# Zero products during the first loads, value copies on another engine, later turns: one edit of a window-attention and expert kernel

## The chip, the cores and the metric

The kernel runs on one core of a Trainium2 chip. The metric is the device time of one execution in microseconds, taken as the median of three runs. Before the change that is 1030.5 us (1030.44 to 1033.13). The core's engines are TensorE (PE), VectorE (DVE), ScalarE (ACT), GpSimd (POOL) and SyncE (SP), which issues most transfers. Each engine works through its own queue in a fixed order and waits on semaphores.

## The reference

The inputs are q, k and v of shape 8 x 8 x 576 x 64 (batch, heads, positions, width), float32, and the weights of one gated expert. What is computed:

```
scores = (q @ k^T) / sqrt(64)        # per batch and head
scores = where(0 <= i - j < 64, scores, -1e9)
attn   = softmax(scores)             # + 1e-9 in the denominator
x      = (attn @ v) as 4608 tokens x 512
xn     = x / sqrt(mean(x*x) + 1e-6) * rms_g
g, val = xn @ w_gate, xn @ w_val     # 512 x 1536 each
out    = (g * sigmoid(g) * val) @ w_out   # 1536 x 512
```

## The kernel before

Tokens are worked in nine tiles of 512. The attention of a batch is done in four pairs of heads (so pairs 0 to 3 are batch 0, 4 to 7 batch 1, 8 to 11 the third batch). The expert's products take each float32 operand as a sum of two f16 parts, three products for one (`three`, lines 790 to 792: high by high, high by low, low by high). Before a weight block can be used it is widened, scaled and split (lines 205 to 236); before a token tile can be used, its high part is cast on ACT (line 746) and its low part is made on POOL (line 748).

The first two batches go through `scores` (line 386 products, line 399 masks on DVE, line 402 exponentials on ACT, lines 469 and 470 sums, lines 474 and 476 scaling on POOL), `weights_to_keys` (line 489 transposes on PE, lines 492 and 494 copies) and `attention_values` (line 507). From the third batch on the scaling and the transpose go another way: POOL moves 32x32 blocks (`move`, line 371, 16 instructions for a pair) and DVE turns them (`turn`, lines 374 and 375), so the turn of a pair waits for its moves.

Values are needed in two layouts, from an even and an odd block. For batch 0 one transfer brings the even layout, and two copies on DVE (lines 342 and 343) make the odd one in the same tile; for later batches two more transfers bring it.

The largest of `rms_g` sets a scale (`rms_weights`, lines 174 to 186): a small transfer, a maximum on DVE (line 175), a PE transpose (`gps`, line 177), another maximum (line 178), and a PE broadcast (`gpb`, line 181).

What stands in which queue when is decided twice. The program emits its parts by planned due times (half steps of the expert's loop; `attention_events` gives those of the attention, and line 598 those of the turns). Then a scheduler that goes by modelled times orders the instructions of each engine. An edit at one place can thus move instructions at others. From tile 1, block 3 on the order is that in which the program emits.

Of the kernel before, what the change touches and what calls it, by code (L numbers as in the profile page):

```python
# [14 lines left out]
F32 = mybir.dt.float32  # L15
F16 = mybir.dt.float16
BF16 = mybir.dt.bfloat16
# [8 lines left out]
P = 128  # L26
B, H, S, D = 8, 8, 576, 64
NPAIR = H // 2
NBLK = S // D
NKT = 5  # L30
# [3 lines left out]
TT = 512  # L34
# [5 lines left out]
NST, T2K, F4K, NKV, NPT, NQ = 3, 8, 6, 3, 3, 3  # L40
LT0, LV0 = 1.4, 2.6
VISITS = (27, 32, 37, 42.5, 47.5)
MOVES = (8.7, 7, 4.5, 4)
FIRST7 = NT
ORDERED = (1, 3)
PREP0, PREP1 = 32.2, 55.5
ST = 2 * NBLK * P - D
# [9 lines left out]
def tile_window_attention_moe(  # L57
# [10 lines left out]
    nc = tc.nc  # L68

    cp = ctx.enter_context(tc.tile_pool(name="cp", bufs=1))  # L70
    wk = ctx.enter_context(tc.tile_pool(name="wk", bufs=2))
# [5 lines left out]
    ps_mo = early.enter_context(tc.tile_pool(name="ps_mo", bufs=3, space=PSUM))  # L77
# [32 lines left out]
    def plus_minus(t):  # L110
        nc.vector.tensor_copy(t[:, 0, :], ident)
        nc.vector.tensor_scalar(t[:, 1, :], ident, -1.0, None, ALU.mult)

    plus_minus(unit)
    one = cp.tile([P, 1], F32, name="one")
    nc.vector.memset(one, 1.0)
    ones = one.to_broadcast([P, P])
# [208 lines left out]
    def load_kv(n):  # L326

        if n == 3:
            kvt = wk.tile([P, 2, NKD, TT], F16, tag="xn", name=f"kv_{n}")
            kvt = kvt.rearrange("p a b c -> p (a b c)").bitcast(F32)[:, : S + NBLK * P]  # L330
        else:
            kvt = wk.tile([P, S + NBLK * P], F32, tag="kv", name=f"kv_{n}", bufs=NKV)
        if n < NPAIR:
            nc.sync.dma_start(out=kvt[:, :S], in_=kv[n, :, :S])
        else:
            nc.sync.dma_start(out=kvt[:, : S + NKT * P], in_=kv[n])
        even = kvt[:, S : S + NKT * P].rearrange("p (u c) -> p u c", c=P)
        odd = kvt[:, S + NKT * P :].rearrange("p (u c) -> p u c", c=P)

        def values_in():  # L340
            nc.sync.dma_start(out=kvt[:, S : S + NKT * P], in_=kv[n, :, S : S + NKT * P])
            nc.vector.tensor_copy(odd[0:D], even[0:D, : NKT - 1, :])
            nc.vector.tensor_copy(odd[D:P], even[D:P, 1:, :])

        if n < NPAIR:
            later[n] = values_in
        else:
            src = kv[n, :, S : S + NKT * P].rearrange("p (u c) -> p u c", c=P)
            nc.sync.dma_start(out=odd[0:D], in_=src[0:D, : NKT - 1, :])
            nc.sync.dma_start(out=odd[D:P], in_=src[D:P, 1:, :])  # L350
        return kvt[:, 0:S], [(odd if j % 2 else even)[:, j // 2, :] for j in range(NBLK)]
# [233 lines left out]
    def attention_events(b, start, pace, tags):  # L585

        load_queries, load_keys, score, to_keys, values, roots, normal, moved, turned = attention(b)
        lk, lv, lq, n0, n1 = tags
        events = ([(n0 - 1, roots)] if b < NRB else []) + [(n0, partial(normal, 0)), (n1, partial(normal, 1))]
        for hp in range(NPAIR):  # L590
            if b >= TB:
                n = NPAIR * b + hp
                i0 = visit_at(n) - half_steps * (b - 1)
                events.append((i0 - 7, partial(load_queries, hp)))
                events.append((i0 - 7, partial(load_keys, hp)))
                for k in range(4):
                    events.append((i0 + (MOVES[hp] + 0.8 * k if n > 11 else 3.5 + 0.4 * k), partial(moved, hp, k)))
                events.append((visit_at(n + 2) - half_steps * (b - 1) - 3, partial(turned, hp)))
                visits[n] = partial(score, hp, 0), partial(values, hp)
                continue  # L600
            i0 = start[2 * hp]
            events.append((i0 - lq, partial(load_queries, hp)))
            events.append((i0 - lq, partial(load_keys, hp)))
            for g in range(2):
                i = start[2 * hp + g]
                events.append((i + lv, partial(values, hp, g)))
                events.append((i + lk, partial(to_keys, hp, g)))
                events.append((i, partial(score, hp, g)))
        return events
# [3 lines left out]
    def visit_at(n):  # L613

        n -= NPAIR * TB
        return VISITS[n] if n < 4 else VISITS[4] + 8 * (n - 4)
# [109 lines left out]
    def normalise(b, xb, ssq, r, piece):  # L726
        cut = TT * (b + 1) - S * b
        for a, z in (((0, cut), (cut, S))[piece],):
# [4 lines left out]
            if t not in xn_tiles:  # L733
                xn = wk.tile([P, 2, NKD, TT], F16, tag="xn", name=f"xn_{t}")
                xn_tiles[t] = xn if t < FIRST7 else operands(t, xn)
            xn = xn_tiles[t]
            rb = broadcast(b, r, a, z) if b < NRB else roots_of_all(b, ssq, a, z)
            for kt in range(NKD):
# [3 lines left out]
                )  # L742
                if t >= FIRST7:
                    continue
# [3 lines left out]
                eng.tensor_tensor(xn[:, 1, kt, o : o + n], x, hi, ALU.subtract)  # L748
            if t >= FIRST7:
                combine(t, xn, xb, a, n // 2, o // 2)  # L750

    def operands(t, xn):

        v = xn.rearrange("p a b c -> p (a b c)").rearrange("p (o a k c) -> p o a k c", o=4, a=2, k=2)
        w = wt[18 + t % 2].rearrange("p o (a k c) -> p o a k c", a=2, k=2)
        last = wt[3 + 4 * (t % 2)][:, 1, :]
        if t == FIRST7:
            last = wk.tile([P, 2 * TT], F16, tag="t2k", name=f"t3_{t}", bufs=T2K)
        last = last.rearrange("p (a k c) -> p a k c", a=2, k=2)
        return {"11": v[:, 0], "21": v[:, 1], "22": v[:, 2], "t4": v[:, 3], "t1": w[:, 0], "t2": w[:, 1], "t3": last, "x1": v[:, 0:2]}  # L760

    def combine(t, ops, xb, a, n, o):

        x11, x21 = xb[:, 0:2, a : a + n], xb[:, 2:4, a : a + n]
        x12, x22 = xb[:, 0:2, a + n : a + 2 * n], xb[:, 2:4, a + n : a + 2 * n]
        t2, t3, t4 = (
            wk.tile([P, TT], F32, tag="t2k", name=f"t{i}_{t}_{a}", bufs=T2K)[:, : 2 * n].rearrange("p (k c) -> p k c", k=2)
            for i in range(3)
        )

        def parts(name, src):
            hi, lo = (ops[name][:, i, :, o : o + n] for i in range(2))
            nc.scalar.copy(hi, src)
            nc.gpsimd.tensor_tensor(lo, src, hi, ALU.subtract)

        parts("11", x11)
        parts("21", x21)
        parts("22", x22)
        nc.vector.tensor_tensor(t3, x22, x12, ALU.subtract)
        nc.vector.tensor_tensor(x12, x11, x12, ALU.subtract)  # L780
        parts("t1", x12)
        nc.vector.scalar_tensor_tensor(t2, x12, -1.0, x22, ALU.mult, ALU.subtract)
        parts("t2", t2)
        parts("t3", t3)
        nc.vector.tensor_tensor(t4, x21, t2, ALU.add)
        parts("t4", t4)
# [111 lines left out]
    def load_sevens(r):  # L898

        if r >= NC * (NT - FIRST7):  # L900
            return
# [7 lines left out]
    def product(t, c, p, acc, first):  # L909
        r = NC * (t - FIRST7) + c  # L910
        o = LEFT[p]
        b = xn_tiles[t][RIGHT[p]]
        w = wt[4 * (r % 3) + o // 2].rearrange("p a (w b k f) -> p a w b k f", w=2, b=2, k=2)[:, o % 2]
        head = None
        for i in range(2):
            with ExitStack() as order:
                if first and i:
                    order.enter_context(tc.issue_after(head))
                for kt in range(2):
                    for j, (l, m) in enumerate(((0, 0), (0, 1), (1, 0))):  # L920
                        at_start = first and i == kt == j == 0
                        nc.tensor.matmul(
                            acc[:, i * HT : (i + 1) * HT],
                            lhsT=w[:, i, l, kt, :],
                            rhs=b[:, m, kt, :],
                            start=at_start,
                            stop=kt == 1 and j == 2,
                            skip_group_check=True,
                        )
                        if at_start:  # L930
                            head = next(x for x in reversed(nc.cur_bb.bb.instructions) if x.engine == nc.tensor.engine)
# [109 lines left out]
    half_steps = 2 * NF + 2 * (TT // P)  # L1041
# [9 lines left out]
    for h, part in attention_events(1, S1, 0, (LK1, LV1, LQ1, 28, 30)):  # L1051
        at_step(h, part)
    if E("S2", None) is not None:
        for h, part in attention_events(2, E("S2", 45), E("P2", 0.8), (E("LK2", 1.5), E("LV2", 2.5), E("LQ2", 4), E("N20", 60), E("N21", 62))):
            at_step(h, part)
# [64 lines left out]
    for t in range(first_full, NTR):  # L1120
# [8 lines left out]
        else:  # L1129
            for c in range(NC):  # L1130
                in_order["on"] |= (t, c) >= ORDERED
                expert_in(t, c)
# [42 lines left out]
```

## Time and profile before

| | |
|---|---|
| median of three runs | 1030.5 us |
| the profiled execution: its own time | 1032.13 us |
| its span, from first to last instruction | 1030.4 us |
| PE busy over the span | 996.0 us (97%) |
| DVE, ACT, POOL busy | 479.4, 409.6, 486.5 us |
| mean granted TensorE clock | 0.985 |

The page gives, for each engine, how long it was busy, and in 40 slices how its busy share went. A clock line tells what TensorE was granted, in tenths of full speed. Idle time of an engine that nothing waits for costs nothing; idle time of PE is what can be won, and so is the time in which it ran at its lower clock.

### The profile page before, as it was taken

To read this page: it belongs to the slowest core of one execution; us is meant where nothing else is said; L and a number is where in the kernel's file an instruction comes from. 1 tells how busy PE (TensorE), PEld (TensorE's weight loads), DVE (VectorE), ACT (ScalarE), POOL (GpSimd) and SP (SyncE) were. 2 spreads that over 40 slices of the span, in tenths; PEclk is the share of its full clock that TensorE was granted. 3 is DMA by queue.
4 is the path that set the end of the run, shared out by engine and by line. 5 is a ranking of instruction groups with operands and counts; after the bars stand their busy time and mean duration, and the time that the engine had idled before them with its cause. 6 is when DMAs were issued, how large, how long until landed. Compare 5 with 4: busy or idle time off the path is not lost.

```text
span 1030.4 us, 16821 instructions
## 1 busy us (share of the span) xinstructions
PE 996.0 (97%) x6443; PEld 499.6 (48%) x6455; DVE 479.4 (47%) x1333; ACT 409.6 (40%) x1066; POOL 486.5 (47%) x634
## 2 busy tenths in 40 slices
PE   7789987999999999999999999999999999999998
PEld 5544544444444445444544454445444444444445
DVE  5688966523374338433743374337533432201220
ACT  5557878234334443334333433443342222212220
POOL 3326644827856576457645764576455022101200
PEclk9989998999999999999999999999999999999999
DMA  7535643011212111211121112111100000000001
GB/s 285 195 107 180 210 158 93 21 35 48 77 57 78 47 47 57 77 47 47 58 77 47 47 57 78 47 47 45 66 2 1 11 31 1 1 21 21 1 1 41
DMA packets 27793, 66.11 MB, mean 64 GB/s; under 512 B 3008, under 2 KB 3264, under 8 KB 27712
## 3 DMA queue, kind: packets, MB, share of 16 engines
q1 hardware_dynamic: 27136, 63.85, 19.1%
q8 instruction: 51, 0.84, 0.3%
q10 hardware_dynamic: 576, 1.18, 0.3%
q14 instruction: 30, 0.25, 0.1%
HBM read 55.58 MB, written 9.44 MB: 63 GB/s over the span
## 4 chain that ended last, share of the span: by engine, by line
PE 84%; DVE 5%; POOL 4%; ACT 4%; DMA 2%; issue 1%; SPq 0%; POOLq 0%; ACTq 0%; DVEq 0%
PE po L791 9%; PE po L792 9%; PE po L790 9%; PE pv L790 8%; PE pg L790 8%; PE pv L792 8%; PE pv L791 8%; PE pg L791 8%; PE pg L792 8%; POOL pm L371 4%; PE sc L386 3%; PE xp L507 2%; PE x L507 2%; DMA kv<-kv 1%; ACT pm L402 1%
## 5 line engine op out<-in xcount | busy, mean ns | idle before, releaser
L371 POOL TENSOR_TENSOR pm<-pm,st 32x288 f32<-32x288 f32 (+1 forms) x384 | 259.1, 675 | 106.9 <-DVE st L428 38.9
L842 POOL TENSOR_TENSOR h<-th,h 128x512 f16<-128x512 f32 x90 | 104.1, 1163 | 175.9 <-ACT h L841 172.7
L839 DVE SCALAR_TENSOR_TENSOR th<-th,pg 128x512 f32<-128x512 f32 x108 | 73.8, 683 | 218.1 <-ACT th L838 218.0
L790 PE MATMUL pv<-xn,wt 128*128 128x512 f16 x432 | 164.9, 382 | 1.9 <-DVE th L839 1.9
L790 PE MATMUL pg<-xn,wt 128*128 128x512 f16 x432 | 164.3, 380 | 1.7 <-ACT wt L235 1.6
L791 PE MATMUL pv<-xn,wt 128*128 128x512 f16 x432 | 164.3, 380 | 0.1
L792 PE MATMUL pv<-xn,wt 128*128 128x512 f16 x432 | 164.2, 380 | 0.1
L791 PE MATMUL po<-wt,h 128*128 128x512 f16 (+1 forms) x436 | 163.5, 375 | 0.8 <-DVE wt L236 0.8
L791 PE MATMUL pg<-xn,wt 128*128 128x512 f16 x432 | 164.0, 380 | 0.0
L792 PE MATMUL pg<-xn,wt 128*128 128x512 f16 x432 | 163.7, 379 | 0.0
L790 PE MATMUL po<-wt,h 128*128 128x512 f16 (+1 forms) x436 | 163.7, 376 | 0.0
L792 PE MATMUL po<-wt,h 128*128 128x512 f16 (+1 forms) x436 | 163.5, 375 | 0.0
L841 ACT CAST h<-th 128x512 f16<-128x512 f32 x105 | 65.0, 619 | 228.2 <-DVE th L840 228.2
L792 PEld LDWEIGHTS <-wt 128*128 128x128 f16 x872 | 85.5, 98 | 102.9 <-issue 1.0
L790 PEld LDWEIGHTS <-wt 128*128 128x128 f16 x872 | 85.4, 98 | 102.5 <-ACT wt L235 1.8
L791 PEld LDWEIGHTS <-wt 128*128 128x128 f16 x872 | 85.7, 98 | 101.6 <-issue 3.2
L838 ACT ACTIVATE th<-pg,hsc 128x512 f32<-128x512 f32 x108 | 74.1, 686 | 102.5 <-PE pg L792 85.1
L840 DVE SCALAR_TENSOR_TENSOR th<-pv,th 128x512 f32<-128x512 f32 x108 | 74.0, 685 | 76.7 <-PE pv L792 76.1
L402 ACT ACTIVATE pm<-pm,st 128x128 f32<-128x128 f32 (+1 forms) x216 | 83.3, 387 | 28.0 <-DVE st L399 27.8
L748 POOL TENSOR_TENSOR xn<-xb,xn 128x64 f16<-128x64 f32 (+7 forms) x63 | 48.9, 806 | 82.7 <-ACT xn L746 82.4
L1003 ACT ACTIVATE ot<-po,hsc 128x512 f32<-128x512 f32 (+1 forms) x37 | 24.9, 674 | 129.3 <-PE po L792 128.9
L792 PEld LDWEIGHTS <-h 128*128 128x128 f16 x436 | 42.9, 98 | 50.0 <-issue 2.1
(144 smaller groups left out, 1090.3 us busy)
## 6 DMA issues: line engine op xcount, KB each, us to landing
kv<-kv SPq DMA_DIRECT2D x28, 608.0 KB, 4.5
out<-ot SPq DMA_DIRECT2D x35, 256.0 KB, 2.0
q<-q SPq DMA_DIRECT2D x28, 288.0 KB, 2.8
kv<-kv SPq DMA_DIRECT2D x56, 128.0 KB, 4.5
st<-w_gate SPq DMA_DIRECT2D x6, 1024.0 KB, 6.4
st<-w_val SPq DMA_DIRECT2D x6, 1024.0 KB, 5.7
st_o<-w_out SPq DMA_DIRECT2D x6, 1024.0 KB, 4.9
kv<-kv SPq DMA_DIRECT2D x4, 320.0 KB, 6.4
```

Of the source, the lines that this page charges most:

```text
L371: nc.gpsimd.tensor_tensor(m[to, :us, fr], p[fr, :us, to], r, ALU.mult)
L402: nc.scalar.activation(part, part, AF.Exp, bias=low, scale=-1.0, accum_out=total)
L507: nc.tensor.matmul(xp[hd, c * D : (c + 1) * D], lhsT=vv[j][rows, hd], rhs=w, start=True, stop=True, skip_group_check=True,)
L748: eng.tensor_tensor(xn[:, 1, kt, o : o + n], x, hi, ALU.subtract)
L790: nc.tensor.matmul(acc, lhsT=lh, rhs=rh, start=first, stop=False)
L791: nc.tensor.matmul(acc, lhsT=lh, rhs=rl, start=False, stop=False)
L792: nc.tensor.matmul(acc, lhsT=ll, rhs=rh, start=False, stop=last)
L838: nc.scalar.activation(th, acc[0], AF.Tanh, scale=th_scale[:, c : c + 1])
L839: nc.vector.scalar_tensor_tensor(th, th, 1.0, acc[0], ALU.add, ALU.mult)
L840: nc.vector.scalar_tensor_tensor(th, acc[1], 2.0**-41, th, ALU.mult, ALU.mult)
L841: (nc.vector.tensor_copy if t < 2 and E('HHE', 'a' * 24)[12 * t + f] == 'v' else nc.scalar.copy)(hh, th)
L842: (nc.vector if t and c == NC - 1 else nc.gpsimd).tensor_tensor(hl, th, hh, ALU.subtract)
```

## The change

There are three edits. Fourteen bf16 products of a tile of zeros (128x128 by 128x512) go to PE ahead of everything else; DVE writes the zeros, and the result is read by nobody. The two copies that make batch 0's odd layout go to POOL instead of DVE. For the third batch the turns are due 0.5 half steps before the visit in which they are used, not 3.

```diff
+WARM = 14
...
+    warm = wk.tile([P, 2 * TT], BF16, tag="t2k", name="warm", bufs=T2K)[:, :TT]
+    nc.vector.memset(warm, 0.0)
+    idle = ps_mo.tile([P, TT], F32, tag="mo", name="idle")
+    for _ in range(WARM):
+        nc.tensor.matmul(idle, lhsT=warm[:, :P], rhs=warm, start=True, stop=True)
...
-            nc.vector.tensor_copy(odd[0:D], even[0:D, : NKT - 1, :])
-            nc.vector.tensor_copy(odd[D:P], even[D:P, 1:, :])
+            nc.gpsimd.tensor_copy(odd[0:D], even[0:D, : NKT - 1, :])
+            nc.gpsimd.tensor_copy(odd[D:P], even[D:P, 1:, :])
...
-                events.append((visit_at(n + 2) - half_steps * (b - 1) - 3, partial(turned, hp)))
+                events.append((visit_at(n + 2) - half_steps * (b - 1) - (3 if n > 11 else 0.5), partial(turned, hp)))
```

In the pieces of order below the number at the end of a name tells buffers apart, and the changed kernel's lines stand 8 later (386 is 394, 489 is 497). First PE's queue at the first transposes of pair 0 (`tr_0_0`), before:

```order
L386 MATMUL sc_1_0_317<-kv_155,q_153 64x128 x4
L386 MATMUL sc_1_1_318<-kv_155,q_153 64x128 x4
L489 MATMUL tr_0_0_250<-ident,p_0_0_193 128x128 x2
L489 MATMUL tr_0_0_250<-ident,p_0_0_193 64x128
L489 MATMUL tr_0_1_257<-ident,p_0_1_194 128x128 x2
L386 MATMUL sc_0_0_365<-kv_162,q_160 64x128 x4
```

The same place on PE in the changed kernel (`gps` and `gpb` belong to `rms_weights`):

```order
L394 MATMUL sc_1_0_334<-kv_172,q_170 64x128 x4
L394 MATMUL sc_1_1_335<-kv_172,q_170 64x128 x4
L394 MATMUL sc_0_0_382<-kv_179,q_177 64x128 x4
L394 MATMUL sc_0_0_382<-kv_179,q_177 64x64
L185 MATMUL gps<-ident,gmx 1x128
L497 MATMUL tr_0_0_267<-ident,p_0_0_210 128x128 x2
L497 MATMUL tr_0_0_267<-ident,p_0_0_210 64x128
L189 MATMUL gpb<-gmx,one 128x1
L497 MATMUL tr_0_1_274<-ident,p_0_1_211 128x128 x2
```

`gps` and `gpb`, which stood behind the first value products, have moved ahead of and in among the first transposes. Next DVE's queue around the maximum of `rms_g`, before; the masks ahead of it (`sc_0_1_366`) are of pair 2:

```order
L399 ISA p_0_1_378,st_0_379<-sc_0_1_366,blocked 128x128
L399 ISA st_0_379 128x1
L175 TENSOR_REDUCE gmx<-gsb 128x1
L469 TENSOR_SCALAR st_0_379<-st_0_379 128x5
L492 COPY pt_1_0_296<-tr_1_0_293 128x256
L470 RECIPROCAL st_0_379<-st_0_379 128x5
L178 TENSOR_REDUCE gmx<-gps 1x1
L179 TENSOR_TENSOR gmx<-gmx,floor 1x1
```

And in the changed kernel; the masks behind it (`sc_1_0_334`) are of pair 1:

```order
L477 TENSOR_SCALAR st_0_293<-st_0_293 128x5
L478 RECIPROCAL st_0_293<-st_0_293 128x5
L183 TENSOR_REDUCE gmx<-gsb 128x1
L186 TENSOR_REDUCE gmx<-gps 1x1
L187 TENSOR_TENSOR gmx<-gmx,floor 1x1
L407 ISA p_1_0_344,st_1_346<-sc_1_0_334,blocked 128x128
L407 ISA st_1_346 128x1
```

The maximum, which waits for the transfer of `rms_g`, has moved ahead of the second half of pair 1's masks, of all of pair 2's, and of the first copies of transposes. Last POOL's queue where the third batch's moves meet the low parts of tile 1 (`xn`), before; the moves are of pair 9 (`pm_2190`) and pair 10 (`pm_2335`):

```order
L371 TENSOR_TENSOR pm_2190<-pm_2190,st_2191 32x9x32 x8
L371 TENSOR_TENSOR pm_2190<-pm_2190,st_2191 32x8x32 x8
L748 TENSOR_TENSOR xn_759<-xb_987,xn_759 128x448 x4
L748 TENSOR_TENSOR xn_2092<-xb_987,xn_2092 128x128 x4
L842 TENSOR_TENSOR wt_99<-th_0_2238,wt_99 128x512
L842 TENSOR_TENSOR wt_99<-th_1_2286,wt_99 128x512
L371 TENSOR_TENSOR pm_2335<-pm_2335,st_2336 32x9x32 x8
```

And in the changed kernel, with pair 9 as `pm_2207` and pair 10 as `pm_2352`:

```order
L379 TENSOR_TENSOR pm_2207<-pm_2207,st_2208 32x9x32 x8
L379 TENSOR_TENSOR pm_2207<-pm_2207,st_2208 32x8x32 x8
L379 TENSOR_TENSOR pm_2352<-pm_2352,st_2353 32x9x32 x8
L379 TENSOR_TENSOR pm_2352<-pm_2352,st_2353 32x8x32 x8
L756 TENSOR_TENSOR xn_776<-xb_1004,xn_776 128x448 x4
L756 TENSOR_TENSOR xn_2109<-xb_1004,xn_2109 128x128 x4
```

Pair 10's sixteen moves have passed the low parts of tile 1. With them its scores have moved on PE, from behind tile 1's third gate product to ahead of tile 0's output products.

## Rows read from the trace of the kernel before

**Rows 1.** The page: busy tenths of PE and its clock in 40 slices.

```profile
PE   7789987999999999999999999999999999999998
PEclk9989998999999999999999999999999999999999
```

**Rows 2.** Busy time by stretch: us; PE, PEld, DVE, ACT, POOL (instructions); clock, DMA share, GB/s.

```profile
4.87:36.26 31.39, 28.83 (x243) 21.28 (x245) 19.24 (x111) 18.90 (x75) 9.99 (x18) 1.00 0.69 245
...
460.00:480.00 20.00, 20.00 (x155) 10.04 (x154) 8.18 (x29) 9.16 (x28) 13.24 (x18) 1.00 0.13 31
```

**Rows 3.** PE groups by form, from three stretches (10:36, 47:58, 84:130); busy us, mean ns.

```profile
L489 PE MATMUL tr<-ident,p 128*128 128x128 f32 x20 | 6.6, 441 | 0.0
...
L715 PE MATMUL rb<-ident,rm 128*128 128x128 f32 x8 | 2.0, 438 | 4.1 <-DVE rm L695 4.1
...
L489 PE MATMUL tr<-ident,p 128*128 128x128 f32 x16 | 3.3, 285 | 0.1
```

**Rows 4.** Timeline of batch 0: start us, us, engine, line; idle before in brackets.

```profile
7.82 0.42 DVE L342 COPY kv<-kv 64x512 f32<-64x512 f32 x1 [5.92 <-DMA kv<-kv]
...
9.50 4.49 PE L386 MATMUL sc<-kv,q 64*64 64x128 f32 x44 [2.46 <-DVE st L399]
...
13.91 1.33 PE L489 MATMUL tr<-ident,p 128*128 128x128 f32 x5
...
15.17 2.57 PE L386 MATMUL sc<-kv,q 64*64 64x128 f32 x26
...
20.52 0.48 PE L507 MATMUL xp<-pt,kv 128*64 128x64 f32 x2
```

**Rows 5.** The transfer of `rms_g`: KB each, us to landing; its issue and reader in the timeline.

```profile
gsb<-rms_g SPq DMA_DIRECT2D x1, 2.0 KB, 10.0
...
8.23 0.50 SPq L174 DMA_DIRECT2D gsb<-rms_g  x1
...
20.00 0.15 DVE L175 TENSOR_REDUCE gmx<-gsb 128x1 f32<-128x4 f32 x1
```

**Rows 6.** POOL in the first 13 us of the timeline.

```profile
2.92 0.34 POOL L145 CAST blocked<-mask 128x192 bf16<-128x192 f32 x1
...
12.36 0.61 POOL L474 TENSOR_TENSOR p<-p,st 128x256 f32<-128x256 f32 x1 [9.09 <-ACT p L402]
```

**Rows 7.** PE's waits over the whole span: us in total, times, longest.

```profile
PE sc L386 <- DMA q<-q: 4.9, 1, 4.9
...
PE tot L673 <- DVE ssq L575: 3.9, 1, 3.9
...
PE x L386 <- DMA kv<-kv: 1.6, 1, 1.6
...
PE x L507 <- DVE st L399: 1.3, 1, 1.3
```

**Rows 8.** Timeline around tile 0's output products and the start of tile 1.

```profile
172.48 28.60 POOL L371 TENSOR_TENSOR pm<-pm,st 32x288 f32<-32x288 f32 x32 [4.20 <-DVE oe L161]
...
178.13 1.44 PE L790 MATMUL po<-wt,h 128*128 128x512 f16 x3
...
204.00 5.55 POOL L748 TENSOR_TENSOR xn<-xb,xn 128x448 f16<-128x448 f32 x8 [2.92 <-ACT xn L746]
...
214.13 0.38 PE L790 MATMUL pg<-xn,wt 128*128 128x512 f16 x1
214.35 0.38 PE L791 MATMUL pg<-xn,wt 128*128 128x512 f16 x1
```

**Rows 9.** Timeline of pair 10's moves and of the turns of pairs 10 and 11.

```profile
234.29 7.06 POOL L371 TENSOR_TENSOR pm<-pm,st 32x288 f32<-32x288 f32 x10 [6.55 <-ACT ssq L570]
...
242.67 3.96 POOL L371 TENSOR_TENSOR pm<-pm,st 32x256 f32<-32x256 f32 x6
...
246.67 1.25 DVE L374 STREAM_TRANSPOSE pm<-pm 128x1024 f32<-128x1024 f32 x1 [2.45 <-POOL pm L371]
...
266.40 1.25 DVE L374 STREAM_TRANSPOSE pm<-pm 128x1024 f32<-128x1024 f32 x1 [2.57 <-POOL pm L371]
```

## The prediction, made before the changed kernel ran

> **What bounds the kernel now.** I read the page's slices first, then busy time by stretch, PE's waits, and the timeline at the places where PE waits or runs slowly. PE is busy 97% of the span, and all its thin slices lie in the first fifth [rows 1]. From about 300 us on PE has no gap, as one such stretch shows [rows 2]; that part does the same products in either kernel, and the change can only make it begin earlier or later. The reader should look for three things ahead of it: PE's idle time, its slow clock, and who ended each wait.
>
> The clock needs care. The page prints full clock from the start. Yet batch 0's 128x128 transposes took 441 ns in the first stretch, the like-sized products of a stretch with a granted clock of 0.50 took 438 ns, and the transposes of a stretch at full clock 285 ns [rows 3]. [...] From 4.87 to 36.26 us it was busy 28.83 of 31.39 us [rows 2]: that half-speed PE, and not the loads, bounds batch 0 once its first wait is over. That wait is 2.46 us before 9.50: DVE stood behind the copy of pair 0's values, which came at 7.82 [rows 4].
>
> [...]
>
> **The change part by part.**
>
> *The zero products.* Three products of that width, at their slowest, took 1.44 us together, and at full speed they follow each other by 0.22 [rows 8]. Fourteen then take between 3.1 and 6.7. Beginning at about 1.2 us, when DVE has written the zeros, they end between 4.3 and 7.9. PE waits 4.9 us for q anyway [rows 7], so the first scores come 0 to 3.0 us later. They have cover: before, DVE came to them behind two copies of 0.42 begun at 7.82 [rows 4], thus at about 8.7. Taken at nothing; without that cover, up to 3.0.
>
> *The copies.* DVE loses eight copies of 0.42 us or more [rows 4], and so the wait for the first values: on its own 2.46 us less at 9.50. POOL gets them. The trace has no such copy on POOL; a cast of 192 elements took 0.34, which gives 0.9 for 512, and the DVE price of 0.42 is the other end. I take 0.9, to which the row on the same engine is nearest. In POOL's new order six copies stand ahead of pair 0's first scaling, which ran at 12.36 [rows 6]. With the first values at 7.8 and the third pair's not taken before 12.65 by DVE, they end between 10.9 and 14.5. That would make pair 0's scaling up to 2 us later, but the next item hides it.
>
> *What the new order does to the maximum of `rms_g`.* This is the largest term. Its transfer is issued at 8.23 and takes 10.0 us to land [rows 5], so it lands at about 18.2, behind the megabytes issued ahead of it; the change touches no load ahead of it. Before, the maximum stood so late in DVE's queue that it ran at 20.00 without a wait [rows 5]. In the changed order it stands ahead of the second half of pair 1's masks, and `gps`, which needs it, stands on PE ahead of the first transposes. Both engines keep their order, so DVE stops there, and PE soon after, until about 18.4. Behind DVE's wait are queued pair 1's and 2's masks, for which ACT waits; behind PE's, everything.
>
> What it costs: before, PE went through the stretch from 13.91 to 21.00 without a gap (five transposes, 26 passes of scores, four transposes, pair 0's first values; the last row ends at 20.52 + 0.48) [rows 4], 7.1 us. Of that the changed order does five score products, ten of the 26 passes, ahead of the wait: 10/26 of 2.57 = 1.0 less. It adds about 0.45 (`gpb` and one score product pulled forward), which later need not be done, and about 0.2 to 0.9 of small waits for the two maxima. So this stretch ends at 18.4 + 7.1 - 1.0 + 0.5 + 0.3 = 25.3, against 21.0; less the 0.45 pulled forward PE is 3.8 late. Some transposes may go closer than in those rows: I take 3.5. Upper end: 4.5, the 18.4 against 13.91 with nothing made good. Lower end: minus 2.5, the wait at 9.50 gone and this one without effect. As PE stays the bound at the lower clock until 36 us, and what follows hangs on it, the 3.5 goes on to the end.
>
> *The middle, 60 to 170 us.* The scheduler swaps neighbours on all engines here, as the low parts of batch 0's last 64 tokens against pair 5's scaling. I find no place where the sign is plain. Taken at 0, with 3 us either way, the size of two of PE's small waits (1.6 and 1.3) [rows 7].
>
> *Pair 10's scores before tile 0's output.* Their 36 passes go from tile 1 to the time ahead of the output products, which began at 178.13 [rows 8]. PE waited 3.9 us there for the sum of squares [rows 7], and pair 10's keys can only be loaded when that sum has freed their buffer. So PE would stand and then do the scores at the lower clock, 36 of 2.57/26 [rows 4], 3.6 us, where full clock would take half. If a quarter of that falls into time in which PE stood anyway, the output products come 2.6 later, and tile 1 is relieved of 1.8. Taken at +0.8, between -1.8 (all in idle time) and +3.6 (none of it, and nothing won later).
>
> *The later turns.* Before, pair 10's turn stood on DVE ahead of pair 11's masks and held them for 2.45 us until POOL's moves were done at 246.67; pair 11's held pair 12's for 2.57 us at 266.40 [rows 9]. PE's two waits after 240, 1.6 for keys and 1.3 behind masks [rows 7], are ends of these chains. In the changed order pair 10's moves are done before tile 1, so pair 11 can go some 2.4 us earlier, and both waits can go. Taken at -2.9; the other end is 0.
>
> Sum: 3.5 + 0 + 0.8 - 2.9 = +1.4. The profiled execution took 1032.13 with a span of 1030.4, so 1.7 lies outside the span and is untouched: 1033.5 for it. It was 1.6 over the median of 1030.5, so for a median I predict 1032.0 (rounded up from 1031.9).
>
> **The rivals.**
>
> *POOL holds tile 1 up (slower).* Pair 10's sixteen moves, 7.06 + 3.96 = 11.0 us where little disturbs them [rows 9], now run ahead of tile 1's low parts. Before, these began at 204.00, the four of 448 columns taking about 1.0 each, and PE wanted the first at 214.35 and the last nine products later, 216.3 at steps of 0.22 [rows 8]. Now: 201.1 (the end of the 28.60) + 11.0 + 4.1 = 216.2, just in time. But moves beside DVE's work are slower: 32 took 28.60, 6.6 over twice 11.0 [rows 8, 9]. If pair 10's lose half as much, 3.3, and its turn start on them is late by 0.5, PE waits 3.7 at tile 1. Price: 1.4 + 3.7 = +5.1, 1035.6. It decides from the moment at which these moves end after 213 on the clock of the kernel before. For it: POOL is then continuously busy for 40 us. Against: early lateness delays PE as well.
>
> *The clock stays up through batch 0 (faster).* If full clock reached from 18.4 to 46 us, PE's half-speed work, from 13.91 to 36.26 less the 1.0 done ahead, 21 us, would shrink towards 11; but ACT, busy 18.90 us of that first stretch [rows 2], has some 15 of these left then, and lets about 6 be won: 1.4 - 6 = -4.6, 1025.9. Against: PE stands idle ahead of 18.4, and in 28.83 us of these float32 products [rows 2] the clock did not rise before.
>
> *The wait for `rms_g` costs nothing (faster).* If the transfer lands earlier, or the freed DVE makes it good, the early term is the -2.5 of the copies: -2.5 + 0.8 - 2.9 = -4.6, also 1025.9. Against it stands the landing time above.
>
> **How the numbers follow.** A measurement of this kernel can tell about 0.3%, 3.1 us, from no change. My forecast has a chance of 0.45 and lies, on its own, between 1029 and 1035: 0.01 faster, 0.33 same, 0.11 slower. The POOL rival has 0.25: 0.03 same, 0.22 slower. The clock rival has 0.13: 0.12 faster, 0.01 same. The last has 0.17: 0.11 faster, 0.06 same. Together: 0.24 faster, 0.43 same, 0.33 slower. The range goes from the two faster rivals' upper part, 1026, to the POOL rival with a bad middle, 1037.
>
> **What would show it.** Right: the changed kernel's DVE idles for some microseconds before the maximum of `rms_g`, ended by its transfer at 18.2; PE's first transposes come after 18.4, with durations near 440 ns; the output products begin about 4 us later; no PE wait between 240 and 300 us. Wrong: transposes of about 285 ns throughout batch 0, first transposes before 15 us, or a PE wait on POOL's low parts at tile 1's first gate product.

## The result and the profile after

The changed kernel takes 1041.17 us (median of four runs, 1039.4 to 1044.46) against 1030.47 us before in the same session: ratio 1.0096, 95% interval 1.0079 to 1.0114. It is slower, and above the range predicted. The profiled execution took 1040.6 us with a span of 1038.8, 8.4 us longer than the span before. The profiled executions stand up to 4 us from the medians of their kernels, so the table further down shows where time goes and the ratios how much. (Medians of the kernel before differ by up to 1.9 us between sessions, so each run below is compared with that kernel in its own.)

The page's slices of the changed kernel, to be held against [rows 1]:

```profile
PE   6879988899999999999999999999999999999998
PEclk7688999899999999999999999999999999999999
```

PE's thin slices still lie in the first fifth. The clock line begins at 7, not 9: in the zero products the clock came up at 6.54 us, fell to 0.50 at 13.37 and stayed there to 40.67, and so the slow stretch is in the record. The low digit is no loss against before, whose 9 stood for a stretch without a record (the first in that trace begins at 36.26), as slow by its transposes as one at a granted clock of 0.50 [rows 3]; batch 0's transposes ran as slowly here (group of PE's line 497 by form, 18.4 to 40 us; busy us, mean ns):

```profile
L497 PE MATMUL tr<-ident,p 128*128 128x128 f32 x20 | 6.8, 444 | 0.0
```

The timeline of the start (start us, us; idle before in brackets), PE and DVE, to be held against [rows 4, 5]:

```profile
1.17 5.83 PE L122 MATMUL idle<-warm 128*128 128x512 bf16 x14 [1.17 <-DVE warm L119]
6.93 1.20 PE L394 MATMUL sc<-kv,q 64*64 64x128 f32 x28
8.65 2.98 PE L394 MATMUL sc<-kv,q 64*64 64x128 f32 x44 [0.52 <-DVE st L407]
...
18.42 0.37 PE L185 MATMUL gps<-ident,gmx 128*1 128x128 f32 x1 [5.86 <-DVE gmx L183]
18.58 0.84 PE L497 MATMUL tr<-ident,p 128*128 128x128 f32 x3
...
18.11 0.16 DVE L183 TENSOR_REDUCE gmx<-gsb 128x1 f32<-128x4 f32 x1 [3.65 <-DMA gsb<-rms_g]
```

DVE stops 3.65 us for the transfer of `rms_g`, PE 5.86 us behind it, and the first transposes come at 18.58 instead of 13.91. POOL's copies and the scaling behind them, to be held against [rows 6]:

```profile
7.71 0.61 POOL L350 COPY kv<-kv 64x512 f32<-64x512 f32 x1 [4.45 <-DMA kv<-kv]
...
12.21 0.61 POOL L482 TENSOR_TENSOR p<-p,st 128x256 f32<-128x256 f32 x1
```

PE's waits over the whole span (total, times, longest), to be held against [rows 7]:

```profile
PE gps L185 <- DVE gmx L183: 5.9, 1, 5.9
...
PE po L799 <- DVE wt L244: 3.2, 1, 3.2
PE sc L394 <- DVE st L407: 3.0, 3, 1.4
PE n L272 <- DVE sq L270: 2.8, 2, 1.7
PE x L515 <- DVE st L407: 2.4, 1, 2.4
...
PE tot L681 <- DVE oe L169: 1.6, 1, 1.6
```

Two of these, for DVE's `sq` and for its last split of the output weight (`wt`), are longer than before, where they read:

```profile
PE n L264 <- DVE sq L262: 1.1, 1, 1.1
...
PE po L791 <- DVE wt L236: 0.8, 1, 0.8
```

And the places of [rows 8, 9]: POOL's moves, now of pairs 8 to 10 in one row, the low parts of tile 1, and the turns of pairs 11 and 12 (by [rows 9] pair 11's stood at 266.40):

```profile
180.67 39.17 POOL L379 TENSOR_TENSOR pm<-pm,st 32x288 f32<-32x288 f32 x48 [5.82 <-DVE st L436]
219.92 5.55 POOL L756 TENSOR_TENSOR xn<-xb,xn 128x448 f16<-128x448 f32 x8
...
269.72 1.25 DVE L382 STREAM_TRANSPOSE pm<-pm 128x1024 f32<-128x1024 f32 x1 [1.51 <-POOL pm L379]
...
289.32 1.25 DVE L382 STREAM_TRANSPOSE pm<-pm 128x1024 f32<-128x1024 f32 x1 [6.44 <-POOL pm L379]
```

Pair 12's turn before:

```profile
282.21 1.25 DVE L374 STREAM_TRANSPOSE pm<-pm 128x1024 f32<-128x1024 f32 x1 [5.26 <-POOL pm L371]
```

How late each kernel is against the one before, at marks that all have (start of the same instruction in the two traces, subtracted). The marks are the scales of weight blocks (line 267, first and third) and a step of the gated products (line 839, the first, ninth, twelfth, 13th, 23rd and 25th):

| mark, us before | after | e3 | e7 | e8 | e1 | e6 | e5 | e9 | e12 |
|---|---|---|---|---|---|---|---|---|---|
| 47.62 | +3.70 | -0.65 | +4.83 | -0.87 | -0.16 | +0.50 | +0.26 | +4.70 | -5.47 |
| 73.66 | +3.77 | -0.57 | +4.90 | -0.79 | -0.36 | +0.30 | +0.07 | +4.71 | -4.79 |
| 93.26 | +6.77 | +0.19 | +7.88 | +0.34 | +5.65 | +3.25 | +0.20 | +4.79 | -6.35 |
| 140.46 | +7.68 | +1.10 | +8.79 | +1.27 | +6.90 | +4.44 | +0.21 | +4.80 | -6.33 |
| 161.44 | +7.61 | +1.20 | +9.01 | +1.40 | +8.50 | +6.17 | +1.12 | +5.34 | -6.50 |
| 217.64 | +8.73 | +4.62 | +12.63 | +4.98 | +10.03 | +8.44 | +0.99 | +5.49 | -6.30 |
| 283.38 | +7.11 | +3.02 | +11.03 | +3.37 | +8.41 | +6.84 | +1.00 | +5.49 | -6.21 |
| 328.33 | +8.49 | +3.02 | +12.63 | +3.37 | +9.98 | +8.20 | +1.00 | +5.49 | -6.21 |

The column of the changed kernel is the whole loss: 3.7 us by 48 us, 3.9 more up to 161, 1.1 more up to 218, 1.6 won and 1.4 lost again behind it. The other columns are the experiments.

### The profile page after: what moved, and what is told of

Its sections match the earlier page's. It is cut to its first block, busy times and chain, and to the rows that moved or that the text cites. A ratio compares the mean times of both kernels' runs of the same rounds, so it can differ in the third digit from the quotient of the medians.

```text
span 1038.8 us, 16845 instructions
## 1 busy us (share of the span) xinstructions
PE 1002.4 (96%) x6457; PEld 501.5 (48%) x6469; DVE 473.8 (46%) x1326; ACT 410.2 (39%) x1066; POOL 488.1 (47%) x642
## 4 chain that ended last, share of the span: by engine, by line
PE 86%; DVE 4%; POOL 3%; ACT 2%; DMA 2%; issue 2%; SPq 0%; POOLq 0%; DVEq 0%; ACTq 0%
PE po L800 9%; PE po L799 9%; PE po L798 9%; PE pv L798 9%; PE pv L799 8%; PE pv L800 8%; PE pg L798 8%; PE pg L800 8%; PE pg L799 8%; PE sc L394 3%; POOL pm L379 2%; PE xp L515 2%; PE x L515 2%; DMA kv<-kv 1%; ACT pm L410 1%
```

## The experiments

Ratios are to the kernel before, with their 95% interval. "Planner" in the expectations is the scheduler. By "rows" I mean rows of PE's order, without the zero products, that stand elsewhere than before: 212 in the changed kernel.

**e1, the zero products alone** (the other two edits undone).

```diff
-            nc.gpsimd.tensor_copy(odd[0:D], even[0:D, : NKT - 1, :])
+            nc.vector.tensor_copy(odd[0:D], even[0:D, : NKT - 1, :])
...
-                events.append((visit_at(n + 2) - half_steps * (b - 1) - (3 if n > 11 else 0.5), partial(turned, hp)))
+                events.append((visit_at(n + 2) - half_steps * (b - 1) - 3, partial(turned, hp)))
```

> The zero products alone; copies back on DVE, turns emitted as before. In this order DVE takes the maximum of rms_g behind the masks, and PE's product for it stands behind batch 0's transposes, as before. Theory A (the early loss of 3.7 us comes from the maximum being ordered ahead and waiting for its transfer; the middle loss of 3.9 us from the order that the first two edits together give): no early wait, so 1030 to 1033 us, whatever the order after 60 us costs. Rival B (the zero products themselves cost: they hold PE back from 6.5 to 13.4 us or move the stretch of half clock): at least half of the changed kernel's loss stands here, 1036 to 1041 us.

1040.54 us, 1.0080 (1.0051 to 1.0109). Theory A fell: the loss is nearly whole without any early wait. It had the start right (-0.16 at 47.62) and overlooked that this order (176 rows) may have a cost of its own, which e6 below tests: 6.0 us come between 74 and 93. One place of it, e1's PE, DVE and POOL:

```profile
87.76 0.61 PE L800 MATMUL pg<-xn,wt 128*128 128x512 f16 x1 [3.00 <-DVE wt L244]
...
84.48 3.23 DVE L244 SCALAR_TENSOR_TENSOR wt<-wt,ws,wt 128x1024 f16<-128x1024 f32 x1
...
84.51 2.12 POOL L238 TENSOR_TENSOR wt<-wt,wt 128x1024 f16<-128x1024 f32 x1 [0.52 <-ACT wt L237]
```

DVE and POOL each make a weight's low part at once, DVE's takes 3.23 us, and PE stands for it.

**e2, the copies alone** (the zero products and the later turns undone; 207 rows).

> The odd-value copies on POOL alone; no zero products, turns as before. Theory A: PE's product for the maximum of rms_g stands 14 rows behind the first transpose (17 in the kernel before), so no early wait, 1029 to 1033 us. Rival C (POOL, slower at these copies and holding up what stands behind them on its queue, is what costs): 1035 to 1041 us.

1032.90 us, 1.0020 (1.0004 to 1.0037): within A, and no support for C. At 47.62 it is 1.13 us ahead, at 217.64 it is 1.43 behind: here too more is lost behind the start than the copies bring. e11 below separates the copies from their order.

**e3, `rms_g` asked for early** in the changed kernel.

```diff
     def rms_weights():
 
-        nc.sync.dma_start(out=gsb, in_=rms_g)
...
             if o[0] == "q":
                 load_queries(i)
+                if i == 2:
+                    nc.sync.dma_start(out=gsb, in_=rms_g)
```

> The changed kernel with one DMA moved: rms_g is asked for on SP right at the first place where its tile exists, ahead of the key and query loads, not behind the second query chunk. The orders of ACT and POOL are those of the changed kernel, PE's and DVE's differ in 2 and 6 small places before 36 us. Theory A: the early wait goes (-3.7 us) and the middle order's 3.9 us stays: 1037 to 1038 us. Rival D (the middle loss is only a consequence of being late): both go, 1031 to 1034 us. Rival E (the transfer was never what held PE back early, or the earlier DMA delays the first loads by as much): 1040 to 1042 us.

1035.76 us, 1.0047 (1.0030 to 1.0064). By the two ratios (1.0096 less 1.0047, of 1031 us) that is 5.0 us less than the changed kernel, so the wait was real. The time is 1 us under A's and 2 over D's, so part of the middle's loss may have gone too; the interval of this difference, about 2.5 us either way, does not decide it. (The expectation has the place wrong: the transfer stands fourth on SP, behind three key and value loads, at 2.1 us instead of 8.10.) The maximum runs without a wait:

```profile
11.86 0.13 DVE L182 TENSOR_REDUCE gmx<-gsb 128x1 f32<-128x4 f32 x1
```

In the table the middle (47.62 to 161.44) costs 1.85 us here, against 3.91 in the changed kernel, in practically the same order. Where the other 2 us lie is seen from 73.66 to 93.26 of the kernel before. The same stretch before, in e3 and in the changed kernel (columns: start and end; us; busy PE, PEld, DVE, ACT, POOL, with instructions; clock, DMA share, GB/s):

```profile
73.66:93.26 19.60, 17.52 (x112) 9.17 (x115) 16.55 (x51) 15.10 (x37) 8.89 (x12) 0.91 0.70 239
```

```profile
73.09:93.45 20.36, 19.43 (x120) 9.80 (x121) 16.75 (x54) 16.38 (x37) 10.57 (x14) 0.92 0.66 227
```

```profile
77.42:100.03 22.61, 20.75 (x118) 10.58 (x121) 17.03 (x53) 16.40 (x37) 9.85 (x14) 0.85 0.63 205
```

The late kernel got the clock's lower level, 0.50, there for 6.83 us (85.04 to 91.87 in the record), the early one for 3.41; e7 and e8 differ in the same way (6.83 and 3.41). At a granted clock of 0.50 those 3.42 us more are, by estimate, 1.7 us of work not done. That the early wait is the reason is not shown: e10 below is the kernel before in its own order, and there the same stretch took 17.95 us at a clock of 1.00, about 1.7 us less than in the execution above, so a difference of this size and kind also stands between two executions of one order.

**e4, the maximum due later** (changed kernel, `'r': 4` for `'r': 2` in the table of due times; 197 rows).

> The changed kernel with one number of the table changed: the due time of the maximum of rms_g is 4 where it was 2. DVE then takes the maximum behind the masks again (as the 70th row, 26 masks ahead of it; 46th with 16 ahead in the changed kernel), PE's product for it behind the first transposes; the order after 60 us is a third one, unlike that of before and that of the changed kernel in some 190 PE rows. Theory A: the early 3.7 us go, so at most 1037.5 us; if a middle order of its own costs nothing 1031 to 1034 us. Rival E (the maximum's place does not matter): 1040 to 1042 us.

1036.37 us, 1.0056 (1.0038 to 1.0073). A held for the early wait, not for an order that costs nothing. The profiled execution is the slowest of its nine (1040.47 us; the fastest 1034.0), 1.00 ahead at 47.62 and 9.99 behind at 217.64: a third order, and it too loses behind the start, though less at the median than in this trace.

After these, two explanations were left for e1: what the zero products do on PE and to the clock, or the order that the scheduler makes when it reckons with them. The next four hold the order fixed and change only what runs. In e6 to e8 it is the same edit to the finished program:

```diff
     with tile.TileContext(nc, schedule_with_timeline_sim=True) as tc:
         tile_window_attention_moe(tc, *args)
+    planned = next(b.instructions for b in nc.main_func.blocks if len(b.instructions) > 1000)
+    zeros = [i for i, x in enumerate(planned) if type(x).__name__ == "InstMatmult"][: WARM - 1]
+    for i in reversed(zeros):
+        del planned[i]
```

**e5, the order of before with the zero products.** They are emitted with `rhs=warm[:, :P]`, and 13 of them get the full 512 columns in `planned`.

> The kernel before, its order of instructions kept on every engine, with the zero products ahead of it on PE: they are planned 128 columns wide (at that width the planner's order of everything else is that of the kernel before), and 13 of the 14 are widened to 512 columns once the order stands. Theory F (the zero products cost through the order that the planner makes when it counts their time; their own time on PE lies in idle time): 1030 to 1033 us, like the kernel before. Rival B (the zero products themselves cost, by their time or by what they do to the clock): 1036 to 1042 us, like the zero products alone in their planned order (1040.5).

1032.76 us, 1.0009 (0.9999 to 1.0019). Theory F holds: all the zero products' own doing is worth about 1 us (between nothing and 2). The trace lacks rows of the 13 widened products, but their weight loads stand there, 0.43 us apart, the last six closer, and the first scores run at the pace of the changed kernel:

```profile
3.71 0.15 PEld L122 LDWEIGHTS <-warm 128*128 128x128 bf16 x1 [0.28 <-issue]
4.05 1.18 PEld L122 LDWEIGHTS <-warm 128*128 128x128 bf16 x6 [0.19 <-issue]
...
5.49 1.20 PE L394 MATMUL sc<-kv,q 64*64 64x128 f32 x28
```

**e6, e1's order without the zero products.**

> The order that the planner made for the zero products alone, kept on every engine, with 13 of the 14 zero products taken out once the order stands. Theory F: the order costs, so 1037 to 1042 us without the products too. Rival B: 1030 to 1034 us.

1040.59 us, 1.0091 (1.0075 to 1.0106), the time of e1. With e5 this settles it: not the products, the order. The collision of e1 does not occur here, though the order is the same; DVE's instruction, 1.2 us ahead of POOL's, takes 1.28 us, and the lag at 93.26 is 3.25 instead of 5.65:

```profile
86.66 1.28 DVE L244 SCALAR_TENSOR_TENSOR wt<-wt,ws,wt 128x1024 f16<-128x1024 f32 x1
...
87.88 2.13 POOL L238 TENSOR_TENSOR wt<-wt,wt 128x1024 f16<-128x1024 f32 x1 [1.72 <-ACT wt L237]
```

**e7 and e8, the orders of the changed kernel and of e3 without the zero products.**

> The changed kernel's order on every engine, with 13 of the 14 zero products taken out once the order stands; the copies on POOL stay. Theory F: the maximum of rms_g still waits for its transfer at 18.2 us and the order of 67 to 170 us is the changed kernel's, so 1037 to 1042 us. Rival B: 1030 to 1034 us; in between, 1034 to 1037 us, each has a share.

> The order of the changed kernel with rms_g asked for early (fourth on SP, behind three loads), and 13 of the 14 zero products taken out once the order stands. Theory F: like the same order with the zero products (1035.8 measured), 1033 to 1038 us. Rival B: 1029 to 1032 us.

1043.51 us, 1.0112 (1.0088 to 1.0135), somewhat above F's range, and 1035.54 us, 1.0037 (1.0025 to 1.0049), within it. By the ratios the early wait costs 7.7 us here, and 5.0 between e3 and the changed kernel, against lags at 47.62 that differ by 5.7 and 4.35. Either excess lies within the interval of its difference, about 2.5 us, so the times alone do not show that the wait costs more than its lag.

**e9, the order of before made late.** Eight reductions stand ahead of one of DVE's copies in `planned`; their results go to a spare tile.

```diff
+    for k in range(8):
+        ...
+        again = mybir.InstTensorReduce(..., outs=[one], ins=list(x.ins), op=r.op, axis=r.axis, ...)
+        planned.insert(at, again)
```

> The kernel before, its order kept on every engine, with DVE held up at the place in batch 0 where the changed kernel waits for rms_g: 8 reductions over 64x512 float32, whose results nobody reads, stand ahead of the third pair's second odd-value copy (13.26 us), by an estimate 8 x 0.55 = 4.4 us (a 64x512 copy takes 0.42). Theory F (the order of 67 to 170 us costs, not lateness): the delay passes through one to one, 1034 to 1036.5 us. Rival D (being late makes the middle worse by itself, as the changed kernel's 3.9 us there against 1.8 in the same order without the early wait may say): 1037.5 to 1040 us. Rival G (later idle time takes the delay up): under 1033 us.

1037.15 us, 1.0045 (1.0030 to 1.0061). The reductions have no rows; they are the gap ahead of the copy:

```profile
17.93 0.42 DVE L345 COPY kv<-kv 64x512 f32<-64x512 f32 x1 [4.88 <-issue]
```

The median lies between F's range and D's. The trace decides for F: the lag stays between 4.70 and 4.80 from 47 to 140 us, so this order passes a delay on one to one, and the 4.8 us over the median of the kernel before in the same session agree; another 0.7 come behind 140 us, where the lower clock held for 6.83 us (from 141.44) instead of 3.41.

**e10, the later turns alone** (the first two edits undone).

> The later turns alone. The planner's order is that of the kernel before, row by row, on all five engines. Theory F: the same time, 1030 to 1032 us. The prediction's own step (the later turns bring 2.9 us): 1027 to 1029 us.

1032.14 us, 1.0001 (0.9992 to 1.0010). The edit changes no row on any engine and brings nothing. So its trace is a second look at the kernel before: 1030.29 us against 1032.13, and 1.66 of the difference lie between 73.66 and 93.26, where the lower clock held for 3.41 us in that execution and not at all in this one.

**e11 and e12, the copies on POOL in nearly the order of before.** One due time, `'s00': 14` for 15, brings the scheduler back to within 24 and 27 rows; e12 has e3's edit as well.

> The copies on POOL, with one number of the table changed (the due time of s00 is 14 where it was 15) so that the planner's order stays near that of the kernel before: 24 PE rows differ, and 5 of them behind the first 280, where the copies alone differed in 207 rows and came to 1032.9 us. Theory F: the copies off DVE bring batch 0 forward by 1.1 us (as the copies alone did at 47.6 us) and the middle gives nothing back: 1028.5 to 1031 us, at or below the kernel before. Rival C (POOL's copies cost by themselves): 1032 to 1036 us.

> As the copies on POOL near the order of before, and rms_g asked for early (fourth on SP, behind three loads), so that DVE's maximum, now in front of the transposes, finds it there; 27 PE rows differ from the kernel before. Theory F: the order is near that of before and nothing waits for rms_g: 1027.5 to 1030.5 us, faster than both kernels. Rival C: 1032 to 1036 us.

1032.40 us, 1.0001 (0.9991 to 1.0010), above F's range, and 1027.46 us, 0.9954 (0.9941 to 0.9966), faster than both kernels. e11 is 1.43 ahead at 47.62 and 0.35 at 73.66: most of it goes where PE waits 5.1 us instead of 4.1 for the tile's roots (`rb` behind DVE `rm`). The copies cost nothing, and alone bring nothing. In e12 the page shows what came:

```profile
PEclk9799998999999999999999999999999999999999
```

```profile
L488 PE MATMUL tr<-ident,p 128*128 128x128 f32 x10 | 2.1, 295 | 1.4 <-ACT pt L491 1.0 <-POOL p L473 0.4
```

From 19.74 to 26.56 us PE had its full clock inside batch 0 (the second row is its transposes there, 295 ns against 441), and the kernel is 5.47 us ahead at 47.62. Of the kernels without zero products, or with one left, only this one got that. Ahead of it PE had one gap, 0.32 us, between 4.47 and 19.74, and DVE found `rms_g` there; in e11 the gap was 0.83, and DVE waited 2.06 us for it. Whether the shorter gap has to do with the rise of the clock, no run shows. Of the further lead at 93.26 (-4.79 to -6.35) the same holds as for e10: the lower clock is missing in that stretch.

## Why the prediction was wrong, step by step

*Zero products, taken at nothing.* Right for the products: +1 us with the interval touching zero (e5). They ended at 7.0, between the 4.3 and 7.9 of the working.

*Copies, taken at nothing on POOL.* Right: 0.61 us each, between the ends 0.42 and 0.9 (0.9 was chosen), and pair 0's scaling came at 12.21 instead of 12.36. PE's wait at 9.50 fell from 2.46 to 0.52. (The lower end of 10.9 for the six copies is not worked out there: six of 0.42 from 7.8 on end at 10.3. Nothing rests on it; they ended at 12.12.)

*The early maximum, +3.5.* Right: +3.70 at 47.62, by the wait foretold (18.11, ended by the transfer). Taking the wait away gave 5.0 us (e3).

*The middle, taken at 0 with 3 either way: this step failed.* It measured +3.9. "No place where the sign is plain" was read as no effect. In the order itself lie, by the traces, about 2 of it (e3 +1.85, e8 +2.27 without the early wait); that this order is slower without the wait and without the zero products is shown by e8's ratio, 1.0037 with 1.0025 as its lower end. The two traces with the wait have the other 2 (+3.91, and e7 +4.18), with twice as long a stretch at the lower clock around 85 us. Whether the wait brings that about is open: two executions of the order of before differ by 1.66 in the same stretch and for the same reason (e10). In the order of before the same lateness cost 0.6 more in the middle (e9). A warning was at hand, 212 rows of PE's order had moved, but no price: the 207 of e2 cost 2.1 us by the ratio.

*Pair 10's scores, +0.8.* The number is right in the changed kernel, +1.1, by luck: the path was another. The scores fell into time in which PE stood anyway (the output products began 7.46 us late, at a lag of 7.61 before them). Inside the output products PE then waited 3.17 us at 199.19, against 0.77 before, for DVE's last split of the output weight, which stood behind pair 8's turn and so behind POOL's moves; the prediction has no such wait. Against it, PE had the lower clock for 1.85 us of the output products instead of 4.90. The other three kernels in this order have the wait too (2.76 to 3.17), got the lower clock once more around its end (e3 193.12 to 196.53, e7 199.16 to 205.99, e8 193.55 to 196.96) and lost 3.4 to 3.6, the forecast's upper end, with the early wait (e7) as without it.

*The later turns, -2.9: this step failed too.* The edit does nothing (e10); what moved pair 10 was the scheduler's answer to the zero products: POOL runs the 48 moves of pairs 8 to 10 in one row in e1, which has only these, and not in e2. Of the two waits of 1.6 and 1.3 that were to go, the first went, and with it the lag fell by 1.6 up to 283. The second stayed and grew to 2.45: the same products, at 286.40 before and 293.51 after, wait for a mask that DVE takes behind pair 12's turn, which POOL's moves held for 6.44 (5.26 before). So it was no end of the chain from pair 10, as the prediction took it to be. It cost nothing more either, for these products began 7.11 late, the lag at 283; the 1.4 that came back came with a stretch at the lower clock (293.26 to 296.67). In e3, which has the same wait and no such stretch, the 1.6 stayed. e1, without the later turns, shows the same fall of 1.6 and the same return.

The sum was 3.5 + 0 + 0.8 - 2.9 = 1.4; it measured 3.7 + 3.9 + 1.1 - 0.2 = 8.5.

*The rivals.* POOL did not hold tile 1 up: the moves ended at 219.84, which less the lag of 8.7 is 211 on the clock of the kernel before, short of the rival's 213; the low parts followed at once, and PE had no gap from 214.90 to 248.90. That the clock would be up through batch 0 no row of before showed, and no run with the zero products does: in the changed kernel it was up from 6.54 to 13.37 us, and for batch 0's transposes it was 0.50 (444 ns each). The wait for `rms_g` did cost.

## What to carry to other kernels

Where a scheduler orders by modelled times, an added instruction is also an edit of the order far behind it. Hold the order fixed and change what runs, or hold what runs and change the order, before saying what an edit costs. Of the orders measured here, the three other ones with 170 rows or more moved (e1, e2, e4) came out slower, as the changed kernel and e3 in nearly its order did, and the two near the old one (e11, e12) equal and faster; so a reordering that wide should not be booked at zero. A small transfer that an early step needs should be asked for ahead of the large ones: it took 5.0 us off the changed kernel, and with the order kept near the old one it made the only gain (e12 beside e11), though part of that came with a rise of the clock whose cause is open. And one trace is one execution: where two traces differ by 2 us, look first at how far two traces of one order do.

## What the runs showed of the hardware

The same split of a weight (128x1024, float32 to f16) took DVE 1.27 to 1.28 us alone and POOL 2.13 to 2.15. Where DVE's began 0.17 to 0.32 us ahead of POOL's, DVE's stayed at 1.26 to 1.28 and POOL's took 2.95 to 3.11; where POOL's had begun 0.20 to 0.49 us ahead, POOL's stayed at 2.13 and DVE's took 2.72 to 3.01. Before:

```profile
97.54 1.26 DVE L236 SCALAR_TENSOR_TENSOR wt<-wt,ws,wt 128x1024 f16<-128x1024 f32 x1
...
97.84 2.96 POOL L230 TENSOR_TENSOR wt<-wt,wt 128x1024 f16<-128x1024 f32 x1 [1.12 <-ACT wt L229]
```

So in these rows the one that comes second pays, and it ends to within 0.2 us where it would if it began at the other's end: DVE's ended at 98.80, 2.13 more make 100.93, and POOL's ended at 100.80. In the changed kernel POOL's ended at 105.62, 1.27 more make 106.89, and DVE's, begun at 103.98, ended at 106.70. At a start 0.03 us apart, DVE's ahead both times, it went either way: in e1 DVE paid (3.23), in e2 POOL did (3.24, with DVE's at 1.28).

With the zero products the changed kernel's clock was up from 6.54 to 13.37 us; then it was 0.50, to 40.67. It fell there while PE stood for `rms_g` (5.86 us); in e3, where PE stood for at most 0.97 us at a time, it fell at 12.21. Batch 0's transposes ran slowly in both: 444 ns each in the changed kernel, and the first five in 1.33 us together in e3, no less than before [rows 4]. Held to the old order the zero products won nothing (e5).
